# Other zero-products before the first product of h, and another order table, in a fused attention and MLP kernel

## The chip, the cores and the metric

The kernel runs on one core of one Trainium2 chip. The metric is the device time of one execution in microseconds. Before the change it is 183.79 us, the median of three runs (183.76 to 183.96). Less is better.

## The reference

The inputs are q, k and v of 8 batches, 8 heads, 576 positions and 64 columns, all in f32, and weights w_in (512 x 1024), w_out (1024 x 512), g_norm and g_ln. What is computed, cut to what matters:

```python
kv = np.einsum('bhsd,bhse->bhde', k, v)
out = np.einsum('bhsd,bhde->bhse', q, kv)
rms = np.sqrt(np.mean(out * out, axis=-1, keepdims=True) + 1e-06)
x = out / rms * g_norm                 # heads side by side: 4608 x 512
...
h = x @ w_in
e = np.exp(h - h_max)
solu = h * e / (np.sum(e) + 1e-09)
ln = (solu - mu) / np.sqrt(var + 1e-06) * g_ln
return ln @ w_out                      # 4608 x 512, f32
```

## The kernel before

The 4608 rows are worked in nine chunks c of 512 rows. Chunks 0 to 7 take eight of every nine positions of one batch each, chunk 8 the positions left over from all batches. A chunk goes through these pieces, by the names of the order table:

- `k`, `v`, `q`: loads from DRAM by GpSimd's DMA queue, with a cast to bf16 (line 281). For the first two batches they are split into parts: `k.0.1` is batch 0, part 1. `q_last` (line 296) loads the left-over positions. `w_in.0`, `w_in.1` (line 302) and `w_out` (line 307) load the weights. There are eight semaphores for these loads; the ninth load takes over the first one's and waits until that has landed, and so on.
- `kv_mm`: the products of k and v on TensorE (line 341); `kv`: their copies out of PSUM on VectorE or ScalarE (lines 191 and 193).
- `qT_mm` and `qT`: transposes of q on TensorE (line 366) and their copies. Later chunks are transposed by DMA instead (`q_turn`).
- `o_mm`: q times kv (line 394). `sq`: squares on ScalarE (line 402). `s_mm`: their means over a head on TensorE (line 408). `ex`, for other chunks `ln` and `ex`: one over the root on ScalarE (lines 422, 412, 416). `x`: the normed rows, on VectorE (line 434). In chunk 0 each of these four comes in four quarters, such as `sq.0.1.0`.
- `h_mm` (line 505, or `ht`, line 568, with rows and columns exchanged for chunks 5 to 8): x times w_in. `exp` or `et` on ScalarE, `u` or `ut` on VectorE, `usq` and `es` (squares of u, sums of e) mostly on GpSimd, `st` for the late chunks on VectorE or ScalarE.
- `sums`, `turn`, `stats`, `rstd`: the statistics of a row.
- `out` (line 696; the last tile in two halves of columns, `out.8.3.0` and `out.8.3.1`, line 705): u times the centred w_out. `ob`: scaled out of PSUM by VectorE or ScalarE (lines 711, 713). `store`: DMA of the result.

Two pieces prepare w_out: `w_mean`, eight products of 512 columns on TensorE that need all of w_out (line 681), and `w_center`, one per block of 128 rows on VectorE (line 684). `table` loads ScalarE's second function table.

`warm` (line 249) multiplies zeros by zeros into a PSUM bank that no one reads. `WARM` lists how many such products each `warm` piece has.

The order of all work is written out by hand in the string `ORDER`, read by `Plan.emit`: each word is a piece; `@dve`, `@act`, `@pool`, `@sp` choose an engine where there is a choice; behind `=` stand the buffers it takes (for a piece that writes PSUM the bank, 0 to 7). Pieces are issued in this order to the queue of their engine, and each engine works its queue in order. Within one engine the table alone decides; between engines, semaphores do.

Of the kernel before, what the change touches and what calls it, by code (L numbers as in the profile page):

```python
# [30 lines left out]
es.0.0=0 h_mm.0.7.0=5 u.0.4.0 exp.0.6.0=3 u.0.3.1 h_mm.0.4.1=2 exp.0.5.1 h_mm.0.5.0=7 usq.0.2@pool exp.0.4.1 u.0.5.1
h_mm.0.6.1=1 usq.0.1@act u.0.6.0 kv_mm.1.0=4 u.0.4.1 q.3.0=0 exp.0.6.1 w_center.1 qT_mm.1.0=0 exp.0.5.0 k.2.0=2
u.0.3.0 kv.1.0.1@act h_mm.0.7.1=2 kv.1.0.0@act qT.1.0@dve=1 exp.0.7.0 out.0.0.0=6 v.2.0=2 u.0.5.0 kv.1.0.2@act
exp.0.7.1 u.0.7.0 es.0.2 o_mm.1.0=04 w_center.6 out.0.2.0=7 sq.1.0.0=1 u.0.7.1 usq.0.5@act w_center.7 s_mm.1.0.0=5
usq.0.7@pool kv_mm.1.1=2 ln.1.0.0=0 u.0.6.1 qT_mm.1.1=3 sq.1.0.1=2 es.0.1 kv.1.1.1@dve kv.1.1.0@dve out.0.2.1
qT.1.1@dve kv.1.1.2@act ex.1.0.0=2 usq.0.4@pool s_mm.1.0.1=1 o_mm.1.1=52 ln.1.0.1=1 x.1.0.0=1 out.0.3.0=3 usq.0.3@pool
sq.1.1.1=0 out.0.0.1 sq.1.1.0=3 es.0.3 ex.1.0.1=0 s_mm.1.1.1=1 s_mm.1.1.0=0 ln.1.1.1=0 out.0.3.1 x.1.0.1 usq.0.6@pool
ln.1.1.0=1 qT_mm.2.0=1 ex.1.1.1=1 qT_mm.3.0=4 q.4.0=1 ex.1.1.0=2 sums.0=0 x.1.1.1 k.3.0=0 qT.3.0@act=2 x.1.1.0 v.3.0=0
qT_mm.2.1=2 turn.0 qT.2.0@act=3 h_mm.1.0=5 stats.0 q.5.0=2 rstd.0 qT.2.1@dve h_mm.1.2=4 q_last.5 exp.1.0=0
ob.0.0@dve=5 h_mm.1.1=0 exp.1.2=2 u.1.0=1 ob.0.3@act=0 qT_mm.3.1=1 ob.0.2@dve=3 kv_mm.2.0=26 exp.1.1 store.0.3 u.1.2  # L40
es.1.0=1 h_mm.1.6=5 kv.2.1.2@act kv.2.0.0@dve kv.2.1.1@act kv.2.0.2@dve kv.2.1.0@act kv.2.0.1@dve u.1.1 o_mm.2.0=37
exp.1.6=1 q_last.6 o_mm.2.1=46 qT.3.1@dve h_mm.1.3=2 sq.2.0.0=1 usq.1.0@pool=1 sq.2.1.1=2 u.1.6 s_mm.2.0.0=0
sq.2.0.1=0 qT_mm.4.0=1 usq.1.1@pool out.0.1.0=5 ln.2.0.0=0 qT.4.0@dve=0 v.4.0=1 exp.1.3 qT_mm.4.1=0 ex.2.0.0=0
s_mm.2.0.1=1 k.4.0=1 u.1.3 out.0.1.1 ln.2.0.1=1 x.2.0.0=2 usq.1.6@pool s_mm.2.1.1=2 sq.2.1.0=3 h_mm.1.4=1 ob.0.1@dve=2
ex.2.0.1=1 es.1.1 s_mm.2.1.0=3 ln.2.1.1=0 h_mm.1.5=5 x.2.0.1 ln.2.1.0=1 q_last.7 qT.4.1@dve h_mm.1.7=2 ex.2.1.1=2
ex.2.1.0=0 out.1.0.0=7 x.2.1.1 exp.1.4=3 x.2.1.0 kv_mm.3.0=30 exp.1.7 u.1.4 h_mm.2.0=6 usq.1.2@act es.1.3 kv.3.0.2@dve
kv.3.1.2@dve h_mm.2.2=4 u.1.7 exp.2.0=0 usq.1.3@pool kv.3.0.0@dve exp.1.5 h_mm.2.4=1 kv.3.1.1@dve kv.3.1.0@dve
exp.2.2=2 k.6.0=2 u.2.0=0 h_mm.2.1=2 exp.2.4=1 kv.3.0.1@dve es.1.2 u.1.5 o_mm.3.0=06 h_mm.2.3=3 u.2.2 sq.3.0.1=1
usq.2.0@pool=0 sq.3.0.0=0 u.2.4 h_mm.2.6=5 exp.2.3 usq.1.5@pool h_mm.2.7=4 exp.2.6=3 u.2.3 exp.2.1 usq.1.4@pool
s_mm.3.0.0=1 u.2.6 out.1.0.1 ln.3.0.0=0 u.2.1 v.6.0=2 exp.2.7 qT_mm.5.0=3 s_mm.3.0.1=5 ex.3.0.0=1 usq.1.7@pool  # L50
qT.5.0@dve=1 h_mm.2.5=1 ln.3.0.1=1 u.2.7 out.1.2.0=2 es.2.0=0 exp.2.5 x.3.0.0=0 ex.3.0.1=2 kv_mm.4.0=35 u.2.5
usq.2.2@pool usq.2.1@act x.3.0.1 o_mm.3.1=40 out.1.3.0=1 sq.3.1.1=2 kv.4.0.0@dve q.7.0=0 kv.4.0.2@dve sq.3.1.0=3
out.1.1.0=6 kv.4.1.1@dve k.5.0=0 kv.4.0.1@dve kv.4.1.0@act kv.4.1.2@act s_mm.3.1.1=3 usq.2.5@pool s_mm.3.1.0=5
out.1.2.1 ln.3.1.0=0 v.7.0=0 ln.3.1.1=1 out.1.3.1 ex.3.1.0=0 q_last.1 out.1.1.1 ex.3.1.1=1 x.3.1.0 v.5.0=1 usq.2.4@act
sums.1=5 x.3.1.1 es.2.2 h_mm.3.4=3 turn.1 usq.2.3@pool stats.1 h_mm.3.0=4 rstd.1 es.2.3 h_mm.3.6=0 ob.1.0@dve=4
exp.3.0=0 es.2.1 ob.1.1@dve=1 exp.3.4=1 store.1.0 h_mm.3.1=5 exp.3.6=3 u.3.0=1 qT_mm.5.1=7 store.1.1 usq.2.7@pool
ob.1.3@act=6 u.3.6 h_mm.3.7=6 qT.5.1@act ob.1.2@dve=7 q.6.0=1 h_mm.3.5=4 u.3.4 exp.3.1 store.1.2 usq.2.6@pool
out.2.3.0=1 exp.3.5 u.3.1 store.1.3 es.3.0=1 exp.3.7 o_mm.4.0=02 u.3.5 o_mm.4.1=73 sq.4.0.0=0 sums.2=5 u.3.7
sq.4.1.0=1 usq.3.0@pool=1 sq.4.0.1=2 s_mm.4.0.0=4 turn.2 out.2.3.1 es.3.3 ln.4.0.0=0 stats.2 s_mm.4.1.0=6 ex.4.0.0=2
out.2.2.0=5 rstd.2 x.4.0.0=1 out.2.1.0=4 ln.4.1.0=1 ob.2.3@dve=0 sq.4.1.1=3 out.2.2.1 ex.4.1.0=0 out.2.0.0=0  # L60
ob.2.2@dve=4 x.4.1.0 s_mm.4.1.1=6 s_mm.4.0.1=1 ln.4.1.1=0 out.2.0.1 ln.4.0.1=1 h_mm.3.3=5 ex.4.0.1=1 kv_mm.5.0=76
ex.4.1.1=2 x.4.0.1 h_mm.3.2=1 ob.2.0@act=1 kv.5.0.2@dve x.4.1.1 kv.5.0.0@act store.2.0 out.2.1.1 kv.5.1.2@dve
exp.3.2=2 qT.6=3 h_mm.4.0=2 u.3.2 exp.3.3 es.3.1 u.3.3 h_mm.4.1=0 exp.4.0=0 kv.5.1.0@act h_mm.4.2=3 u.4.0=0
usq.3.2@act qT.7=2 kv.5.1.1@dve usq.4.0@pool=0 ob.2.1@act=7 h_mm.4.4=1 kv.5.0.1@dve exp.4.2=3 h_mm.4.5=5 es.3.2
exp.4.1 exp.4.4=2 h_mm.4.3=2 store.2.3 u.4.1 usq.3.3@pool exp.4.5 u.4.4 o_mm.5.0=67 store.2.1 kv_mm.6.0=40 u.4.5
sq.5.0.0=0 usq.3.7@pool out.3.1.0=1 exp.4.3 kv.6.1.1@dve usq.4.1@pool sq.5.0.1=1 u.4.3 h_mm.4.6=5 u.4.2 usq.4.4@pool
h_mm.4.7=2 exp.4.6=1 kv.6.1.2@dve kv.6.0.2@dve es.4.0=0 usq.3.1@act kv.6.1.0@dve s_mm.5.0.0=3 out.3.1.1 u.4.6
usq.3.5@act kv.6.0.0@dve s_mm.5.0.1=0 usq.3.6@pool ln.5.0.0=1 kv.6.0.1@dve out.3.0.0=5 exp.4.7 usq.3.4@pool
out.3.2.0=4 ln.5.0.1=0 u.4.7 ex.5.0.0=0 out.3.0.1 usq.4.6@pool ex.5.0.1=1 x.5.0.0=2 o_mm.5.1=30 q_last.4 sums.3=2
x.5.0.1 sq.5.1.0=3 sq.5.1.1=2 k.7.0=1 s_mm.5.1.0=6 usq.4.7@act turn.3 es.4.1 out.3.3.0=7 stats.3 ln.5.1.0=1 out.3.2.1  # L70
ex.5.1.0=2 es.4.3 s_mm.5.1.1=2 rstd.3 x.5.1.0 out.3.3.1 ln.5.1.1=0 q_last.0 ob.3.1@dve=6 ht.5.0.0=6 ob.3.0@act=1
usq.4.2@pool ex.5.1.1=0 store.3.0 ht.5.1.0=3 et.5.0.0=00 q_last.3 x.5.1.1 ht.5.0.1=2 q_last.2 et.5.1.0=3 ut.5.0.0=1
ht.5.1.1=1 usq.4.3@pool et.5.0.1 ut.5.1.0 ht.5.3.0=5 et.5.1.1 ob.3.3@dve=0 es.4.2 ht.5.2.0=0 ut.5.0.1 et.5.3.0=1
usq.4.5@pool ht.5.3.1=6 ut.5.1.1 et.5.2.0=2 ut.5.3.0 uT.5.0=1 ht.5.2.1=3 et.5.3.1 ut.5.2.0 o_mm.6.1=72 et.5.2.1
o_mm.6.0=15 ut.5.3.1 sums.4=0 sq.6.1.0=0 ut.5.2.1 store.2.2 sq.6.0.0=1 ob.3.2@dve=7 out.4.1.0=6 sq.6.1.1=3 turn.4
s_mm.6.1.0=3 stats.4 out.4.2.0=4 uT.5.1 ln.6.1.0=1 st.5.2@dve=1 sq.6.0.1=2 s_mm.6.0.0=0 out.4.3.0=3 ln.6.0.0=0
st.5.0@dve=0 out.4.2.1 ex.6.0.0=1 ex.6.1.0=2 s_mm.6.0.1=0 x.6.0.0=0 out.4.3.1 rstd.4 x.6.1.0 out.4.1.1 ob.4.2@act=1
st.5.1@dve=1 ln.6.0.1=0 store.4.2 s_mm.6.1.1=1 ht.6.1.1=7 ln.6.1.1=1 st.5.3@dve=0 qT.8=0 ex.6.0.1=0 ht.6.0.0=4
ex.6.1.1=1 ht.6.0.1=0 x.6.0.1 et.6.0.0=01 x.6.1.1 ht.6.1.0=1 store.0.0 ob.4.3@dve=4 ht.6.2.0=5 et.6.1.0=3 ut.6.0.0=1
# [733 lines left out]
```

## Time and profile before

| | |
|---|---|
| median of three runs | 183.79 us |
| profiled execution, its own time | 184.49 us |
| its span, first to last instruction | 182.7 us |
| TensorE busy | 174.1 us, 95% |
| ScalarE busy | 146.1 us, 80% |
| VectorE busy | 127.1 us, 70% |
| GpSimd busy | 89.8 us, 49% |
| mean granted clock of TensorE | 0.98 |

The profile is of one execution. PE is TensorE's products, PEld its weight loads, DVE is VectorE, ACT ScalarE, POOL GpSimd, SP the engine that issues stores. L249 is line 249 of the kernel. In an answer by lines, "x48" is a count, and the mean of one follows in ns. A product's busy time includes its way through the array, so back-to-back products overlap; how often they start is read from groups that follow each other without a gap. The granted clock is TensorE's, 1.00 for full speed.

### The profile page before, as it was taken

How to read it: one execution, taken by the hardware profiler on the slowest of the kernel's cores; microseconds unless marked ns; L12 is line 12 of the kernel's file. 1: busy time of each engine (PE TensorE's matmuls, PEld its weight loads, DVE VectorE, ACT ScalarE, POOL GpSimd, SP SyncE). 2: the span in 40 equal slices, each digit the busy share in tenths (PEclk: the TensorE clock that was granted, in tenths of full speed). 3: DMA queues.
4: the chain of work that ended last, by engine and by line, in shares of the span. 5: the costliest groups of instructions: out<-in, count | busy, mean ns of one | idle time of the engine just before them, and what ended most of it. 6: DMA issues, size and time to landing. Idle time of an engine off the chain costs nothing.

```text
span 182.7 us, 4909 instructions
## 1 busy us (share of the span) xinstructions
PE 174.1 (95%) x1969; PEld 89.2 (49%) x1969; DVE 127.1 (70%) x298; ACT 146.1 (80%) x289; POOL 89.8 (49%) x104
## 2 busy tenths in 40 slices
...
GB/s 23 197 243 387 204 205 206 207 209 166 184 233 195 200 151 148 207 218 277 70 170 178 58 58 179 134 171 117 173 202 207 112 147 199 189 129 209 199 214 216
DMA packets 48551, 32.83 MB, mean 180 GB/s; under 512 B 28936, under 2 KB 43024, under 8 KB 48528
## 3 DMA queue, kind: packets, MB, share of 16 engines
...
q10 hardware_dynamic: 288, 0.39, 0.6%
...
## 4 chain that ended last, share of the span: by engine, by line
PE 89%; ACT 3%; DMA 3%; POOL 1%; issue 1%; DVE 1%; POOLq 0%
PE out_ps L696 32%; PE h_ps L505 19%; PE ht_ps L568 15%; PE kv_ps L341 4%; PE s_ps L408 4%; PE qT_ps L366 3%; PE sum_ps L652 3%; DMA q_sb<-in_q_dram 3%; PE warm_ps L249 3%; PE o_ps L394 3%; ACT osq_sb L402 2%; PE mean_ps L681 1%; PE acc_ps L705 1%; ACT lss_sb L412 1%; POOL v_sb L281 0%
## 5 line engine op out<-in xcount | busy, mean ns | idle before, releaser
L434 DVE SCALAR_TENSOR_TENSOR x_sb<-o_ps,g_rep,rst_sb 128x512 bf16<-128x512 f32 x36 | 26.0, 747 | 19.8 <-ACT rst_sb L416 15.1
L696 PE MATMUL out_ps<-w_out_sb,u_sb 128*128 128x512 bf16 x160 | 39.2, 379 | 0.0
L505 PE MATMUL h_ps<-x_sb,w_in_sb 128*128 128x512 bf16 (+1 forms) x192 | 37.4, 344 | 0.0
L531 POOL TENSOR_TENSOR usq_sb<-u_sb 128x512 bf16<-128x512 bf16 x31 | 31.9, 1042 | 4.9 <-DVE u_sb L520 4.8
L537 POOL TENSOR_TENSOR es_sb<-e_sb 128x512 bf16<-128x512 f32 x20 | 25.4, 1276 | 12.3 <-ACT e_sb L513 12.3
L513 ACT ACTIVATE e_sb<-h_ps,zero_t 128x512 f32<-128x512 f32 (+1 forms) x48 | 27.7, 621 | 4.0 <-PE h_ps L505 3.6
L520 DVE TENSOR_TENSOR u_sb<-h_ps,e_sb 128x512 bf16<-128x512 f32 (+1 forms) x48 | 27.2, 596 | 4.9 <-ACT e_sb L513 4.5
L568 PE MATMUL ht_ps<-w_in_sb,x_sb 128*128 128x512 bf16 x128 | 29.3, 379 | 0.2 <-ACT lss_sb L412 0.2
L696 PE MATMUL out_ps<-w_out_sb,usq_sb 128*128 128x512 bf16 x120 | 28.5, 379 | 0.0
L505 PEld LDWEIGHTS <-w_in_sb 128*128 128x128 bf16 x192 | 18.2, 98 | 15.0 <-issue 0.7
L578 ACT ACTIVATE e_sb<-ht_ps,zero_t 128x512 f32<-128x512 f32 x32 | 21.9, 692 | 3.6 <-PE ht_ps L568 2.8
L402 ACT ACTIVATE osq_sb<-o_ps,zero_t 128x512 bf16<-128x512 f32 x36 | 23.2, 689 | 1.6 <-PE o_ps L394 1.6
L696 PEld LDWEIGHTS <-u_sb 128*128 128x128 bf16 x160 | 15.2, 98 | 17.4 <-issue 0.6
L412 ACT ACTIVATE lss_sb<-s_ps,eps_t 128x512 f32<-128x512 f32 x32 | 21.6, 694 | 2.3 <-PE s_ps L408 2.2
L586 DVE SCALAR_TENSOR_TENSOR u_sb<-ht_ps,e_sb 128x512 bf16<-128x512 f32 x32 | 21.2, 686 | 2.1 <-ACT e_sb L578 1.8
L416 ACT ACTIVATE rst_sb<-lss_sb,zero_t 128x512 f32<-128x512 f32 x32 | 22.2, 733 | 0.2
L568 PEld LDWEIGHTS <-x_sb 128*128 128x128 bf16 x128 | 12.5, 98 | 15.6 <-issue 0.7
L696 PEld LDWEIGHTS <-usq_sb 128*128 128x128 bf16 x120 | 11.5, 98 | 13.5 <-issue 0.2
L193 DVE CAST kvd<-kv_ps 64x128 bf16<-64x128 f32 (+1 forms) x31 | 8.5, 287 | 13.2 <-PE kv_ps L341 12.8
L597 DVE SCALAR_TENSOR_TENSOR es_sb<-u_sb 128x1024 bf16<-128x1024 bf16 x13 | 15.5, 1218 | 0.0
L191 ACT CAST kvd<-kv_ps 64x128 bf16<-64x128 f32 (+1 forms) x17 | 4.5, 263 | 13.7 <-DVE kvd L193 11.6
L713 DVE TENSOR_SCALAR rooms<-out_ps,rstd 128x512 f32<-128x512 f32 x18 | 13.3, 745 | 1.8 <-PE out_ps L696 1.0
...
## 6 DMA issues: line engine op xcount, KB each, us to landing
...
w_out_f<-in_moe_w_out_dram POOLq DMA_DIRECT2D x1, 2048.0 KB, 12.2
...
```

The source lines that it names most:

```text
L402: nc.scalar.activation(out=t[:, :], in_=T[("o", *i)].rearrange("p a b c -> p (a b c)"), func=AF.Square, bias=zero_t[:, :])
L412: nc.scalar.activation(out=t[:, :], in_=T["s", i][:, :], func=AF.Ln, bias=eps_t[:, :])
L416: nc.scalar.activation(out=t.rearrange("p a b c -> p (a b c)"), in_=T["lss", i][:, :], func=AF.Exp, scale=-0.5, bias=zero_t[:, :])
L434: nc.vector.scalar_tensor_tensor(out=dst, in0=T["o", c, hf, z][:, :, :, :], scalar=g_rep[:, :], in1=T["rst", (c, hf, z)][:, :, :, :], op0= ...
L505: nc.tensor.matmul(t[:, :], w_in_sb[:, dt, f * 128:(f + 1) * 128], T["x", c][:, dt, cols_of(g)], start=(dt == 0), stop=(dt == NP - 1),)
L513: nc.scalar.activation(out=T["e", c, f // 2][:, f % 2, cols_of(g)], in_=T["h", c, f, g][:, :], func=AF.Exp, bias=zero_t[:, :])
L520: nc.vector.tensor_tensor(out=T["u", c][:, f, cols_of(g)], in0=T["h", c, f, g][:, :], in1=T["e", c, f // 2][:, f % 2, cols_of(g)], op=MUL)
L531: of(engine).tensor_tensor(out=dst, in0=src, in1=src, op=MUL)
L537: nc.gpsimd.tensor_tensor(out=T["es", c][:, n, :], in0=e[:, 0, :], in1=e[:, 1, :], op=ADD)
L568: nc.tensor.matmul(t[:, :], T["x", c][:, dt, 128 * m:128 * m + 128], w_in_sb[:, dt, 512 * w:512 * w + 512], start=(dt == 0), stop=(dt == N ...
L578: nc.scalar.activation(out=T["e", c, m][:, w, :], in_=T["ht", c, m, w][:, :], func=AF.Exp, bias=zero_t[:, :], accum_out=T["acc", c][:, 2 * ...
L696: nc.tensor.matmul(T["out", c, m][:, :], u_rows(c, f, m), w_out_sb[:, f, :], start=(f == 0), stop=(f == NF - 1),)
```

## The change

All 28 zero-products in 18 pieces become 44 in 9 pieces, and the whole order table is replaced. Nothing else is edited; the instructions that compute the result are the same in number.

```diff
-    WARM = (7, 2, 2, 2, 2, 1, 1, 1, 1, 1, 1, 1, 1, 1, 1, 1, 1, 1)
+    WARM = (14, 13, 2, 1, 1, 2, 5, 2, 4)
```

The table up to the first products of h:

```diff
-warm.0=7 v.0.0=0 k.0.0=0 q.0.0=0 ident k.0.1 q.0.2 v.0.1 q.0.1 q.0.3 w_out=01234567 warm.1=7 warm.2=7 qT_mm.0.0=0
-turn_g=1 w_in.0 w_in.1 k.1.0=1 warm.3=7 warm.4=7 qT_mm.0.2=2 kv_mm.0.0=3 v.1.0=1 kv.0.0.0@dve qT.0.0@dve=0
-kv.0.0.2@act warm.5=7 warm.6=7 kv_mm.0.1=4 q.1.0=1 qT.0.2@dve g_mean qT_mm.0.1=5 kv.0.1.2@act k.1.1 kv.0.1.0@act
-kv.0.0.1@dve qT.0.1@dve qT_mm.0.3=6 v.1.1 o_mm.0.0.0=70 qT.0.3@act kv.0.1.1@act warm.7=5 warm.8=5 o_mm.0.0.1
-o_mm.0.1.0=21 sq.0.0.1=0 o_mm.0.1.1 sq.0.0.0=1 sq.0.1.1=2 warm.9=4 warm.10=4 warm.11=4 s_mm.0.0.0=3 ex.0.0.0=0
-s_mm.0.1.1=5 s_mm.0.0.1=6 sq.0.1.0=3 x.0.0.0=0 ex.0.1.1=1 warm.12=4 warm.13=4 s_mm.0.1.0=4 ex.0.0.1=2 warm.14=7
-w_mean=3 q.1.1 ex.0.1.0=0 x.0.0.1 table x.0.1.0 x.0.1.1 w_center.5 warm.15=0 warm.16=2 warm.17=2 h_mm.0.0.0=7
...
+warm.0=7 v.0.0=0 ident v.0.1 q.0.0=0 k.0.0=0 k.0.1 q.0.2 q.0.3 q.0.1 w_out=01234567 w_in.0 w_in.1 warm.1=7 kv_mm.0.0=0
+v.1.0=1 qT_mm.0.0=1 kv.0.0.0@act qT.0.0@dve=0 kv.0.0.1@dve warm.2=7 kv_mm.0.1=2 k.1.0=1 qT_mm.0.2=3 q.1.0=1
+kv.0.1.1@act kv.0.0.2@act qT.0.2@dve kv.0.1.0@act warm.3=1 o_mm.0.0.0=45 v.1.1 turn_g=6 kv.0.1.2@act qT_mm.0.3=7
+qT_mm.0.1=1 k.1.1 qT.0.3@dve o_mm.0.1.0=03 qT.0.1@dve g_mean warm.4=2 o_mm.0.0.1 o_mm.0.1.1 sq.0.0.0=0 sq.0.1.1=1
+warm.5=1 s_mm.0.0.0=2 ex.0.0.0=0 sq.0.1.0=2 x.0.0.0=0 sq.0.0.1=3 warm.6=6 s_mm.0.1.0=7 ex.0.1.0=1 s_mm.0.0.1=1
+s_mm.0.1.1=6 x.0.1.0 ex.0.1.1=2 warm.7=4 w_mean=2 q.1.1 x.0.1.1 table x.0.0.1 w_center.7 w_center.2
+warm.8=5 h_mm.0.0.0=4 q.3.0=2 w_center.5 h_mm.0.2.0=7 exp.0.0.0=0 h_mm.0.2.1=6 w_center.4 exp.0.2.0=1 h_mm.0.0.1=0
...
```

On TensorE, 11 zero-products stood ahead of the first real product before (the transposes `qT_mm.0.0`); now 27 stand ahead of it (`kv_mm.0.0`). The other 17 are spread between there and the first `h_mm` in both tables. On GpSimd the eight loads of batch 0 that come ahead of w_out are in another order, with `ident` second instead of fourth. Behind `w_in.1` the loads of batch 1 begin with v instead of k, then `q.3.0` comes ahead of `q.2.0`, and `v.2.0` now stands ahead of the first `usq`.

From there on the same pieces follow in another order, with other banks and here and there another engine. The end of the table:

```diff
-store.7.3 rstd.8 out.8.0.1 ob.8.1@act=4 store.7.2 out.8.2.0=4 ob.8.0@act=3 out.8.3.0=5 store.8.0@sp out.8.2.1
-ob.8.3.0@dve=5 store.8.3.0@sp out.8.3.1=0 ob.8.2@act=2 store.8.1@sp store.8.2@act ob.8.3.1@dve store.8.3.1@act
+store.7.2 out.8.2.0=3 ob.7.3@dve=1 ob.8.1@dve=5 out.8.3.0=4 store.7.3 store.8.1@act out.8.2.1 ob.8.3.0@dve=4
+store.8.3.0@act out.8.3.1=2 ob.8.2@dve=0 store.8.2@act ob.8.3.1@dve store.8.3.1@sp
```

More of the change, by code (lines that the diff above doesn't have):

```diff
@@ L31 @@
[L31 to L79, printed above, removed]
-store.3.3 ht.6.3.0=2 stats.5 et.6.1.1 ut.6.1.0 out.5.2.0=3 et.6.0.1 ut.6.1.1 out.5.3.0=4 et.6.2.0=1 ut.6.0.1 rstd.5
@@ new lines @@
+usq.0.4@pool ln.1.1.1=1 qT_mm.3.1=7 ex.1.1.0=0 qT_mm.3.0=0 q.4.0=1 ex.1.1.1=1 sums.0=5 x.1.1.0 v.3.0=0 qT.3.0@act=2
+x.1.1.1 k.3.0=0 qT_mm.2.0=2 turn.0 h_mm.1.6=1 stats.0 v.4.0=1 qT.3.1@dve rstd.0 q_last.5 h_mm.1.0=0 qT.2.0@dve=3
+ob.0.0@act=7 h_mm.1.2=5 ob.0.3@dve=2 exp.1.0=0 ob.0.2@act=5 qT_mm.2.1=7 u.1.0=1 h_mm.1.1=2 exp.1.2=1 qT.2.1@dve
+exp.1.6=2 u.1.2 kv_mm.2.0=43 exp.1.1 h_mm.1.3=6 kv.2.1.1@dve kv.2.0.1@act es.1.0=1 kv.2.0.0@dve kv.2.1.0@act
+kv.2.0.2@dve kv.2.1.2@act u.1.6 o_mm.2.1=07 exp.1.3 o_mm.2.0=53 q.5.0=2 u.1.1 out.0.1.0=4 sq.2.1.1=0 k.4.0=1
@@ new lines @@
+sq.3.1.0=3 usq.2.4@pool s_mm.3.1.1=0 s_mm.3.1.0=7 ln.3.1.1=0 out.1.2.1 k.6.0=0 ln.3.1.0=1 es.2.3 out.1.1.0=0
+ex.3.1.0=2 sums.1=7 ex.3.1.1=0 usq.2.7@pool x.3.1.0 x.3.1.1 out.1.1.1 v.6.0=1 turn.1 usq.2.1@pool stats.1 h_mm.3.4=1
+rstd.1 es.2.1 h_mm.3.0=4 usq.2.3@act ob.1.3@dve=0 kv.4.1.1@act h_mm.3.6=7 ob.1.1@dve=1 store.1.3 exp.3.0=0
+usq.2.5@pool h_mm.3.7=3 u.3.0=1 exp.3.6=1 usq.2.2@pool ob.1.0@dve=3 usq.2.6@act h_mm.3.5=0 u.3.6 exp.3.4=3 q_last.7
+store.1.0 qT_mm.5.1=4 exp.3.7 u.3.4 h_mm.3.1=6 q.6.0=1 kv.4.1.2@act store.0.0 exp.3.5 kv.4.1.0@dve sums.2=7 u.3.7
```

82 lines of the change are left out of this document (61 added, 21 removed).

## The prediction

> **What bounds the kernel now.** I read the page first, then the chain of waits from its end backwards, then the body as one stretch, then the landings of the loads and the clock by stretches.
>
> ```profile
> PE 174.1 (95%) x1969; PEld 89.2 (49%) x1969; DVE 127.1 (70%) x298; ACT 146.1 (80%) x289; POOL 89.8 (49%) x104
> ```
>
> TensorE is busy for 95% of the span, far more than any other engine, so the question is where its other 5% lie and whether its busy time is work at its best rate. The chain of waits (start, length, what) answers both:
>
> ```profile
> 15.22 0.34 PE qT_ps L366 x4
> 15.56 0.02 issue
> 15.59 0.44 DVE qT_sb L193
> ...
> 17.16 1.85 ACT osq_sb L402 x3
> ...
> 20.36 0.39 PE s_ps L408
> 20.75 0.22 PE warm_ps L249
> 20.96 1.84 PE mean_ps L681 x8
> 22.80 0.46 PE warm_ps L249 x2
> 23.27 0.04 issue
> 23.31 0.38 PE warm_ps L249
> 23.69 6.64 PE h_ps L505 x60
> ...
> 166.05 10.36 PE out_ps L696 x48
> ...
> 178.15 0.89 PE acc_ps L705 x8
> ```
>
> Up to the first product of h the chain goes back and forth between ACT, TensorE and loads; from there on it stays on TensorE nearly throughout. 48 products of 512 columns take 10.36 us there, 216 ns each, with no gap between them. The stretch from the first h (its instruction starts at 23.52 in the timeline quoted below) to the end of the last product (178.15 + 0.89, about 179.03):
>
> ```profile
> 23.52:179.03 155.51, 155.30 (x1809) 80.46 (x1807) 120.49 (x274) 137.21 (x274) 75.22 (x78) 1.00 0.97 175
> ```
>
> In 155.51 us TensorE is busy 155.30 (the columns are length, then PE, PEld, DVE, ACT, POOL, the clock, DMA). So the body is its products back to back, at full clock (1.00). The time of the kernel is then (start of the first h) + 155.5 + the tail, 182.7 - 179.03 = 3.7 us. Another order of the same products cannot shorten the body by more than that 0.2 us and the small cost of changing shapes; what it can do is start the body sooner, or put waits into it.
>
> **The change part by part.** *The head.* The first h needs three things: w_in's first half, x's first two quarters, and, by its place behind w_mean on TensorE, w_out. When do they land?
>
> ```profile
> L307 POOL DMA_DIRECT2D w_out_f<-in_moe_w_out_dram x1: 944/944/944, 7.9 to 7.9; - x1
> ...
> DMA to landing us min/median/max: 12.2/12.2/12.2
> ```
>
> ```profile
> L302 POOL DMA_DIRECT2D w_in_sb<-in_moe_w_in_dram x1: 804/804/804, 8.8 to 8.8; - x1
> ...
> DMA to landing us min/median/max: 13.3/13.3/13.3
> ```
>
> w_out is here at 7.9 + 12.2 = 20.1, w_in.0 at 8.8 + 13.3 = 22.1. In both tables the same eight loads with the same bytes, and ident, stand ahead of w_out on POOL's queue, only permuted. So these two landings stay, give or take 0.2 us. Before, w_mean did not start at 20.1: TensorE came to it only behind the last s_mm, which waited for a square on ACT until 20.36, and a zero-product. From there, 8 products of w_mean took 1.84 us and three zero-products with their waits 0.88 (22.80 to 23.69).
>
> Is TensorE ready for w_mean by 20.1 in the changed table? Its first product is kv_mm.0.0, which needs the first and the fourth load; the last of the eight is q.0.1. The fourth and the eighth load of before had the same bytes ahead of them:
>
> ```profile
> L281 POOL DMA_DIRECT2D k_sb<-in_k_dram x1: 713/713/713, 4.4 to 4.4; - x1
> ...
> DMA to landing us min/median/max: 5.5/5.5/5.5
> ```
>
> ```profile
> L281 POOL DMA_DIRECT2D q_sb<-in_q_dram x1: 748/748/748, 7.2 to 7.2; - x1
> ...
> DMA to landing us min/median/max: 6.2/6.2/6.2
> ```
>
> So kv_mm.0.0 can start at 9.9 and the last transposes of q at 13.4. The 27 zero-products now ahead of kv_mm.0.0 fit in front of it:
>
> ```profile
> 1.20 4.65 PE L249 MATMUL warm_ps<-zeros 128*128 128x512 bf16 x11 [1.20 <-DVE zeros L212]
> 8.60 0.61 PE L366 MATMUL qT_ps<-ident,q_sb 128*128 128x128 bf16 x4 [2.75 <-DMA q_sb<-in_q_dram]
> ...
> 23.52 0.71 PE L505 MATMUL h_ps<-x_sb,w_in_sb 128*128 128x256 bf16 x5
> ```
>
> Eleven of them took 4.65 us, 423 ns each, twice the 216 of the body. If the clock comes after about 3.6 us, 8 slow and 19 fast ones end at 1.2 + 3.4 + 4.1 = 8.7; if all 27 stayed slow, at 12.6. I take 8.7 to 10.5, so between no delay and 0.6 us.
>
> From 13.4 on: four transposes and the copy on DVE took 0.34 and 0.44 us in the chain; with some 0.6 for waits and the sixteen small products of o_mm (an estimate; they are shorter than the 216 ns products) ACT's first square starts near 14.8 to 14.9. ACT then has eight operations in a row, four squares and four rsqrts. Three squares took 1.85 us in the chain, with 0.69 for the last to finish, so 0.58 apart. The fifth of the eight is the last square and ends near 14.9 + 4 x 0.58 + 0.69 = 17.9; its s_mm and two zero-products bring TensorE to w_mean at 18.7. The eighth ends near 19.7 and the x that waits for it (0.75 on DVE, by the 745 ns of the last row quoted in this part) at 20.5, ahead of h. So TensorE now waits 1.4 us for w_out, and all delays in the head up to 1.4 us are covered by that wait. That the first 27 zero-products, the earlier ident on POOL and the later k.0.0 cost nothing rests on this cover; without it each would count in full.
>
> Then: w_mean starts at 20.15, 1.84 us, four zero-products of warm.8 at 216 ns, 0.86 us: 22.85 to 22.9. w_in.0 has been there since 22.1. The first h starts at 22.9 instead of 23.52: **0.6 us gained**. Bounds: 0 (TensorE at w_mean only at 20.75 again) and 0.85 (w_out 0.2 earlier).
>
> *The body.* The same products, so 155.5 us. POOL now issues v.2.0 ahead of its first usq, and that load waits until an earlier one has landed, since it takes over its semaphore; es and the other usq queue behind it. POOL is busy 75 of 155 us in the body, and what it makes is first needed by sums of batch 0, so this is hidden; uncovered it is one issue, 0.71 us. Which places of the new order leave ACT (137 of 155 us busy) or DVE (120) late I bound from the rows: at best the idle 0.2 us of the stretch vanishes, at worst two operations of ACT (0.69 each) come late in full, 1.4 us. I take 0, since nearest to the row of before.
>
> *The tail.* ob.8.2 moves from ACT to DVE, between the two halves of ob.8.3.
>
> ```profile
> 179.06 0.48 DVE L713 TENSOR_SCALAR rooms<-acc_ps,rstd 128x256 f32<-128x256 f32 x1 [1.20 <-PE acc_ps L705]
> ```
>
> ```profile
> L713 DVE TENSOR_SCALAR rooms<-out_ps,rstd 128x512 f32<-128x512 f32 x18 | 13.3, 745 | 1.8 <-PE out_ps L696 1.0
> ```
>
> Its product ends at 178.15, where acc_ps begins in the chain, and DVE stood idle for 1.20 us before 179.06; 0.745 fits in with 0.1 to spare. Cost 0; if not covered, up to 0.5 us. The last store leaves from SP instead of ACT, taken as equal.
>
> *Sum.* 182.7 - 0.6 + 0 + 0 = 182.1 us of span. The profiled execution took 184.49 us by its own time, 1.8 around its span, and the median of the runs is 183.79, 0.7 below it. The difference carries over: **183.79 - 0.6 = 183.2 us**.
>
> **The rivals.** *A, the body starts no sooner (about 183.8).* For it: k.0.0 is now the fourth load instead of the second, and the chain behind it (kv, copies, o_mm, squares) has to make up 2 us. Against it: before, nothing used that early landing; kv_mm.0.0 stood behind two transposes and ran at half clock, and ACT's squares began only at 17.16. It takes a slip of 1.4 us before the gain begins to shrink and 2.0 before it is gone.
>
> *B, slower: the clock falls while TensorE waits for w_out.* By stretches of before (length, PE busy and count, and so on; the clock is the number behind POOL):
>
> ```profile
> 4.82:8.24 3.42, 0.97 (x4) 0.20 (x2) 0.00 (x0) 0.00 (x0) 3.42 (x6) 1.00 1.24 193
> 8.24:11.65 3.41, 3.00 (x13) 1.42 (x13) 0.00 (x0) 0.00 (x0) 3.41 (x5) 0.50 1.27 202
> 11.65:15.07 3.42, 3.36 (x77) 2.16 (x74) 2.00 (x6) 0.26 (x1) 2.64 (x4) 0.50 1.32 346
> ```
>
> A stretch with 0.97 us of work in 3.42 was followed by half clock; the next, with 3.00, did not end it, and the one with 3.36 did (the stretch of the body above stands at 1.00). The changed kernel's 3.4 us up to 20.2 hold perhaps 1.9 us by the same records (four s_mm and some five zero-products, each with its row longer than its 216 ns), between the first of these and the last. If the clock falls there, 3.4 us of w_mean, warm.8 and the first h run at half speed and lose 1.7 us: 183.2 + 1.7 = 184.9. It decides from 0.6 us lost, that is, from 1.2 us at half clock. The Trainium skill, "TensorE: Matmul & The Clock Gate" (Why this matters for your kernels), asks for no idle gap over about 3 us; by it the gap of 1.4 us is harmless, B would have no chance, and the time would stay at 183.2. The trace does not quite agree: the gap in which the clock fell here was 2.75 us long (the bracket of the row at 8.60), below that figure. So I leave B one chance in ten.
>
> *C, slower: the new order makes ACT or DVE late in the body.* ACT's 137 of 155 us leave little room and where one operation is late TensorE's queue stands behind it. Against it: the old order, as dense, leaves TensorE idle for 0.2 us only. At 1.4 us: 183.2 + 1.4 = 184.6; it decides from 0.6 us of waits.
>
> **How the numbers follow.** Forecast 0.58, A 0.20, B 0.10, C 0.12. The forecast's own range is 182.6 to 183.5 (0.85 to 0.3 gained in head and body). About 0.2%, 0.37 us, is what can be told from no change here. The forecast is nearly all below that line; A is no change; B and C are slower: faster 0.58, same 0.21, slower 0.21. To leave out no more than two in ten the range goes from 182.5 to 184.5, which takes in A and the lighter half of C.
>
> **What would show it right or wrong.** Right: TensorE idle for about 1.4 us ahead of mean_ps, released by the DMA of w_out_f near 20.1; the first h at 22.9; full clock from the first stretch on; some 155.5 us from the first h to the last product; 3.7 us behind it. Wrong: squares on ACT starting after 16.5; a clock of 0.50 anywhere between 16 and 25; h not before 23.4; named waits of TensorE in the body adding up to over 0.6 us.

## The result and the profile after

| | before | after |
|---|---|---|
| median of the runs, us | 183.77 | 186.49 |
| profiled execution, its own time, us | 184.49 | 185.57 |
| its span, us | 182.7 | 183.8 |
| first h, us | 23.52 | 22.98 |
| end of the last product, us | 179.03 | 178.44 |
| tail behind it, us | 3.67 | 5.36 |
| mean granted clock | 0.98 | 1.00 |

The changed kernel is slower by 1.4%: ratio 1.0141, 95% interval 1.0103 to 1.0179. Its profiled execution is the fastest of its runs, 0.9 us below their median, so part of the loss does not stand in this trace at all. The ratios of all kernels leave out three executions that were over 1.5% above the fastest of the same kernel: 187.24 and 187.33 us with the gap filled, 186.53 us with ident back (both kernels are described below).

First the head, from the timeline of TensorE in the changed kernel (start, length, what; in brackets the idle time ahead of it and what ended it):

```profile
7.66 1.89 PE L248 MATMUL warm_ps<-zeros 128*128 128x512 bf16 x8
11.28 0.75 PE L340 MATMUL kv_ps<-v_sb,k_sb 64*64 64x64 bf16 x36 [1.73 <-DMA k_sb<-in_k_dram]
...
16.84 0.38 PE L407 MATMUL s_ps<-osq_sb,head_mean 128*128 128x512 bf16 x1
...
20.15 2.11 PE L680 MATMUL mean_ps<-w_out_f,g_mean 128*128 128x512 f32 x8
22.11 1.04 PE L248 MATMUL warm_ps<-zeros 128*128 128x512 bf16 x4
22.98 1.25 PE L504 MATMUL h_ps<-x_sb,w_in_sb 128*128 128x256 bf16 x10
```

The first h is where it was forecast (22.98 against 22.9), and behind w_out's landing, as forecast. But the gap is in another place: TensorE stands for 1.73 us ahead of kv_mm.0.0, because k.0.0 landed at 11.2 and not at 9.9, and not for 1.4 us ahead of w_mean. The chain of waits in the changed kernel has both ends of this:

```profile
4.39 6.84 DMA k_sb<-in_k_dram
...
20.18 2.09 PE mean_ps L680 x8
```

TensorE comes to w_mean at 20.18 instead of the forecast 18.7, just behind w_out's landing at 20.1. The late k.0.0 has used up the whole cover of 1.4 us, and the first h is on time with nothing to spare.

The body and the tail, as stretches (length, then PE, PEld, DVE, ACT, POOL busy, clock, DMA share, GB/s), in the changed kernel:

```profile
22.98:178.44 155.46, 155.35 (x1809) 80.21 (x1807) 121.53 (x271) 137.12 (x276) 76.86 (x80) 1.00 0.96 174
```

```profile
178.44:183.80 5.36, 0.00 (x0) 0.00 (x0) 0.48 (x1) 0.00 (x0) 0.00 (x0) 0.93 0.55 185
```

and the tail of the kernel before:

```profile
179.03:182.70 3.67, 0.00 (x0) 0.00 (x0) 0.48 (x1) 0.00 (x0) 0.00 (x0) 0.95 0.52 193
```

The body is 155.46 us, the forecast's 155.5. Behind it the changed kernel still has 5.36 us x 185 GB/s = 0.99 MB to move, the kernel before 3.67 x 193 = 0.71. The 0.28 MB between them are about two DMAs of 128 KB. The queue of SP in the changed kernel shows where they come from:

```profile
164.23 4.14 SPq L743 DMA_DIRECT2D out_dram<-rooms  x6
168.47 2.12 SPq L601 DMA_TRANSPOSE usq_sb<-u_sb  x1
170.69 4.15 SPq L743 DMA_DIRECT2D out_dram<-rooms  x6
174.93 0.54 SPq L738 DMA_DIRECT2D out_dram<-rooms  x1
175.58 2.66 SPq L743 DMA_DIRECT2D out_dram<-rooms  x4
178.99 0.34 SPq L725 DMA_DIRECT2D out_dram<-rooms  x1
```

and in the kernel before:

```profile
165.22 3.67 SPq L744 DMA_DIRECT2D out_dram<-rooms  x6
168.99 2.08 SPq L602 DMA_TRANSPOSE usq_sb<-u_sb  x1
171.57 5.04 SPq L744 DMA_DIRECT2D out_dram<-rooms  x8
176.70 0.54 SPq L739 DMA_DIRECT2D out_dram<-rooms  x1
```

L743 (L744 before) is a store of chunks 0 to 7, two DMAs of 128 KB each. By the two tables, the eight DMAs that SP issues in the kernel before from 171.57 on are the four stores of chunk 7. In the changed kernel ten are issued from 170.69 on, and two more just ahead of the transpose: among them are store.5.3 at 173.6, whose rows were ready since 135.9, and store.5.1 at 167.1 (ready since 137.5). SP issues one in some 0.6 us, so the four cost it 2.4 us, and the last DMA of chunk 7 leaves at 177.4 instead of 176.0. ACT issues its own stores at 176.4, 177.3 and 178.4 into the same stretch. What this makes of the transfers, by the rows of the last stores in the changed kernel:

```profile
L743 SPq DMA_DIRECT2D out_dram<-rooms x4: 486/567/847, 175.6 to 177.4; - x4
...
DMA to landing us min/median/max: 2.8/3.0/4.5
```

and in the kernel before:

```profile
L744 SPq DMA_DIRECT2D out_dram<-rooms x5: 548/587/592, 173.4 to 176.0; - x5
...
DMA to landing us min/median/max: 2.3/2.4/2.4
```

From issue to landing the slowest takes 4.5 us instead of 2.4.

### The profile page after: what moved, and what is told of

Same layout as the page of the kernel before. It is cut to its first block, busy times and chain, and to the rows that moved or that the text cites. A ratio compares the mean times of both kernels' runs of the same rounds, so it can differ in the third digit from the quotient of the medians.

```text
span 183.8 us, 4936 instructions
## 1 busy us (share of the span) xinstructions
PE 174.7 (95%) x1985; PEld 89.7 (49%) x1985; DVE 129.0 (70%) x295; ACT 145.8 (79%) x291; POOL 90.6 (49%) x105
## 4 chain that ended last, share of the span: by engine, by line
PE 86%; ACT 4%; DMA 4%; POOL 2%; issue 1%; DVE 0%; POOLq 0%
PE out_ps L695 32%; PE h_ps L504 19%; PE ht_ps L567 15%; PE s_ps L407 4%; PE kv_ps L340 4%; DMA k_sb<-in_k_dram 4%; PE sum_ps L651 3%; PE qT_ps L365 3%; PE o_ps L393 3%; ACT osq_sb L401 3%; PE warm_ps L248 1%; PE mean_ps L680 1%; PE acc_ps L704 1%; POOL v_sb L280 1%; ACT lss_sb L411 1%
## 5 line engine op out<-in xcount | busy, mean ns | idle before, releaser
L504 PE MATMUL h_ps<-x_sb,w_in_sb 128*128 128x512 bf16 (+1 forms) x192 | 36.6, 344 | 0.0
L530 POOL TENSOR_TENSOR usq_sb<-u_sb 128x512 bf16<-128x512 bf16 x32 | 32.8, 1042 | 0.8 <-PE h_ps L504 0.7
L401 ACT ACTIVATE osq_sb<-o_ps,zero_t 128x512 bf16<-128x512 f32 x36 | 22.8, 688 | 1.6 <-PE o_ps L393 1.5
L712 DVE TENSOR_SCALAR rooms<-out_ps,rstd 128x512 f32<-128x512 f32 x24 | 17.5, 747 | 7.9 <-PE out_ps L695 6.4
L415 ACT ACTIVATE rst_sb<-lss_sb,zero_t 128x512 f32<-128x512 f32 x32 | 22.5, 728 | 0.5
L411 ACT ACTIVATE lss_sb<-s_ps,eps_t 128x512 f32<-128x512 f32 x32 | 21.4, 691 | 1.8 <-PE s_ps L407 1.3
L695 PEld LDWEIGHTS <-usq_sb 128*128 128x128 bf16 x120 | 11.6, 98 | 14.2 <-DVE x_sb L433 0.6
L192 DVE COPY qT_sb<-qT_ps 128x1024 bf16<-128x1024 bf16 (+1 forms) x13 | 7.7, 604 | 12.3 <-PE qT_ps L365 12.3
L190 ACT CAST kvd<-kv_ps 64x128 bf16<-64x128 f32 (+1 forms) x25 | 6.5, 260 | 12.0 <-PE kv_ps L340 11.7
L248 PE MATMUL warm_ps<-zeros 128*128 128x512 bf16 x44 | 13.1, 438 | 1.3 <-DVE zeros L211 1.2
## 6 DMA issues: line engine op xcount, KB each, us to landing
q_sb<-in_q_dram POOLq DMA_DIRECT2D x6, 512.0 KB, 11.6
```

The source lines that it names most:

```text
L401: nc.scalar.activation(out=t[:, :], in_=T[("o", *i)].rearrange("p a b c -> p (a b c)"), func=AF.Square, bias=zero_t[:, :])
L411: nc.scalar.activation(out=t[:, :], in_=T["s", i][:, :], func=AF.Ln, bias=eps_t[:, :])
L415: nc.scalar.activation(out=t.rearrange("p a b c -> p (a b c)"), in_=T["lss", i][:, :], func=AF.Exp, scale=-0.5, bias=zero_t[:, :])
L504: nc.tensor.matmul(t[:, :], w_in_sb[:, dt, f * 128:(f + 1) * 128], T["x", c][:, dt, cols_of(g)], start=(dt == 0), stop=(dt == NP - 1),)
L530: of(engine).tensor_tensor(out=dst, in0=src, in1=src, op=MUL)
L695: nc.tensor.matmul(T["out", c, m][:, :], u_rows(c, f, m), w_out_sb[:, f, :], start=(f == 0), stop=(f == NF - 1),)
```

## The experiments

The twelve kernels ran in three groups of four, each with its own runs of the kernel before on the same chip: medians 184.03, 184.21 and 183.98 us. Ratios are to those.

### The same kernel again, and the two stores early

The first kernel is the changed one, not edited. In the second two words are moved:

```diff
-... out.7.3.0=1 store.5.1 st.8.0@act=0 ...
-... rstd.8 store.5.3 out.8.1.1 ...
+... store.4.0 store.5.1 store.5.3 x.7.1.0 ...
```

> The changed kernel once more, unedited, for a second trace and the scatter of its runs: its profiled span was 183.8 us, but the other runs had 184.6 to 184.9. Theory (the tail): the last product of TensorE again ends near 178.4, the first h again starts near 23.0, and the span differs from run to run by what lies behind the last product (5.3 us in the trace at hand, 3.7 before). Rival (the clock or the head): in a slower run the first h starts later than 23.0, by the half-speed time, and the tail stays at 5.3 us or below.

> The changed kernel with the stores of batch 5 that its table puts among the last ones (store.5.1 and store.5.3, four DMAs of 128 KB) moved up behind store.4.0, where the issuing engine stands idle from 142 to 148 us. Theory (stores pile up in the tail): with 256 KB and 1.2 us of issues less behind 173.6 us, the tail falls from 5.3 to about 3.7 us, the profiled span to about 182.1 us, and the time by at least 1.1 us, to 185.4 or below; to 183.2 if the slower runs too come from there. Rival (the head or the body costs the time): the tail may shrink, but the time stays within 0.4 us of 186.5.

Measured: the same kernel 186.64 us, ratio 1.0130 (1.0106 to 1.0153). Its profiled execution is again the fastest of its runs, 185.51 us. In it the first h starts at 23.38, 0.4 us later than in the first trace, at full clock and behind w_out's landing at 20.5; the last product ends at 178.83, and the tail is 4.90 us. The slower executions left no trace, so theory and rival are not decided by this kernel.

With the two stores early the time is 185.31 us, 1.0073 (1.0053 to 1.0092). The stretch behind the last product there:

```profile
179.75:183.49 3.74, 0.00 (x0) 0.00 (x0) 0.48 (x1) 0.00 (x0) 0.00 (x0) 0.94 0.50 168
```

The tail is back at 3.74 us and 3.74 x 168 = 0.63 MB, and the time falls by 186.64 - 185.31 = 1.3 us. So the two stores cost that. But the kernel is still slower than before by 0.7%, and its first h comes only at 24.29: there is a second loss, in the head.

### Heads exchanged

The pieces and zero-products up to the first h are taken from the one kernel and all behind them from the other, with some PSUM banks renamed: the kernel before with the changed head, and the changed kernel with the head of before.

```diff
-warm.0=7 v.0.0=0 k.0.0=0 q.0.0=0 ident k.0.1 q.0.2 ... w_mean=3 ... warm.17=2 h_mm.0.0.0=7
+warm.0=7 v.0.0=0 ident v.0.1 q.0.0=0 k.0.0=0 k.0.1 ... w_mean=3 ... warm.8=2 ... h_mm.0.0.0=7
```

> The kernel before with the changed kernel's order up to the first product of h (44 zero-products, the loads in the new order; bank numbers exchanged where the two tables collide) and its own order from there on. Theory: the head gains and the rest of the table loses, so the first h starts at 23.0 instead of 23.5 and the time falls by about 0.5 us, to 183.2 to 183.4. Rival (the zero-products cost the time): 184.5 or more.

> The changed kernel with the order of before up to the first product of h (28 zero-products, the loads in the old order) and the new order from there on. Theory: the body and the tail are those of the changed kernel, and they start 0.5 us later: 187.0 us, tail still over 5 us. Rival (the new head costs the time): near 183.8 us.

Measured: the kernel before with the changed head 184.85 us, 1.0040 (1.0021 to 1.0060): the head that was to gain 0.6 us loses 0.8. That is the rival's number, but not its cause: the kernel with the loads back, below, has the same 44 zero-products and is no slower than the kernel before. The changed kernel with the old head 186.08 us, 1.0098 (1.0072 to 1.0123), tail 5.97 us. That is 0.6 us less than with its own head, where 0.5 us more was expected. What happens in the changed head is seen by its stretches. The clock changes only at steps of 3.41 us. Here are stretches cut at those steps: first the kernel before with the changed head, the stretch with the gap ahead of kv_mm.0.0 and the next,

```profile
7.73:11.14 3.41, 1.21 (x6) 0.36 (x4) 0.00 (x0) 0.00 (x0) 2.65 (x4) 1.00 1.14 177
11.14:14.56 3.42, 3.04 (x75) 2.50 (x78) 0.72 (x2) 0.27 (x1) 2.39 (x4) 0.50 1.36 272
```

then the same two in the kernel with the stores early,

```profile
8.96:12.38 3.42, 1.53 (x44) 1.00 (x43) 0.00 (x0) 0.15 (x1) 2.20 (x3) 1.00 1.18 170
12.38:15.79 3.41, 3.05 (x54) 1.82 (x52) 1.14 (x3) 1.16 (x5) 2.65 (x4) 0.50 1.33 319
```

and in the profiled execution of the changed kernel:

```profile
8.97:12.38 3.41, 1.68 (x44) 1.07 (x43) 0.00 (x0) 0.27 (x1) 2.20 (x3) 1.00 1.28 191
12.38:15.79 3.41, 3.38 (x73) 2.12 (x72) 1.97 (x6) 1.04 (x4) 2.81 (x4) 1.00 1.31 364
```

With 1.68 us of products in the stretch the clock stays, with 1.53 it is halved for the whole next one. The gap ahead of kv_mm.0.0 is 2.23, 1.89 and 1.73 us long in these three, and the last two lie on either side of the edge, so the head is not the same from one execution to the next. The Trainium skill, "TensorE: Matmul & The Clock Gate" (Part 1: The HAM clock gate), describes such a free-running window of 3413 ns, and the stretches agree with it. The advice of the Trainium skill, "TensorE: Matmul & The Clock Gate" (Why this matters for your kernels), to leave no idle gap over about 3 us, is not strict enough here: a gap of 1.89 us cost the clock.

What the fall costs can be read from the mean granted clock that every execution has on record. In the traces it is 0.995 or more where the clock did not fall in the head, and 0.991 or less where it did. Of the twelve executions of the kernel before with the changed head, six have 0.995 or more and took 184.2 to 184.8 us; six have 0.990 or less and took 184.9 to 186.1, by the medians 0.8 us more. So in that kernel a fallen clock goes with some 0.8 us more.

The clock is not the whole loss of the head, though. The changed kernel has eight executions without a trace in its two sets of runs. Four of them have 0.997 or more and took 186.4 to 187.0 us, four have 0.982 to 0.985 and took 186.4 to 186.7; the two with a trace, both at full clock, took 185.6 and 185.5. What makes those eight some 1 us slower is not shown. One candidate stands in the trace with the stores early, in the weight load of w_mean (PEld):

```profile
21.44 1.70 PEld L678 LDWEIGHTS mean_ps<-w_out_f,g_mean 128*128 128x128 f32 x8 [0.38 <-DMA w_out_f<-in_moe_w_out_dram]
```

There w_out itself landed only at 21.4, so that first h at 24.29 would have come hardly earlier at full clock. In the kernel before with the changed head w_out was there at 20.6 and nothing waited for it; its first h at 24.10 is late by the clock.

### The loads, ident and the gap

Three kernels on top of the one with the two stores early. In the first the loads of batch 0 go back to about the order of before, in the second ident alone does, in the third the gap is filled by more zero-products:

```diff
-warm.0=7 v.0.0=0 ident v.0.1 q.0.0=0 k.0.0=0 k.0.1 q.0.2 q.0.3 q.0.1 w_out=01234567
+warm.0=7 v.0.0=0 k.0.0=0 q.0.0=0 ident v.0.1 k.0.1 q.0.2 q.0.3 q.0.1 w_out=01234567
```

```diff
-warm.0=7 v.0.0=0 ident v.0.1 q.0.0=0 k.0.0=0 k.0.1
+warm.0=7 v.0.0=0 v.0.1 q.0.0=0 ident k.0.0=0 k.0.1
```

```diff
-    WARM = (14, 13, 2, 1, 1, 2, 5, 2, 4)
+    WARM = (14, 22, 2, 1, 1, 2, 5, 2, 4)
```

> The changed kernel with store.5.1 and store.5.3 behind store.4.0 again, and with the loads of batch 0 as v.0.0 k.0.0 q.0.0 ident v.0.1 k.0.1 q.0.2 q.0.3 q.0.1. Theory (the head is lost where k.0.0 lands behind the fill, because ident stands second): k.0.0 lands at about 7.9 as in the kernel before, kv_mm.0.0 starts where the fill ends, 9.5 to 9.8, with no wait of over 0.5 us ahead of it and no fall of the clock; w_out lands at about 20.1, the first h starts at 22.9, the last product ends at 178.4, the tail is 3.7: span 182.1, and the time 0.4 to 0.7 us below the kernel before. Rival (the landing of w_out sets the head, and it comes late whatever the order of the small loads is when the batch-0 loads are crowded by other work): w_out lands at 20.5 to 21.4, h at 23.3 to 24.3, time 0 to 1.3 us above the kernel before.

> The changed kernel with the two stores early, and ident moved from second to fourth place, the loads else in the changed order. Theory (ident alone delays every small load behind it by 1.2 us): the second load lands at 7.9 instead of 9.1, k.0.0 at 9.95 instead of 11.2, kv_mm.0.0 starts at 10.0 after a wait of about 0.4 us, no fall of the clock; w_out at 20.1, h at 22.9, time 0.4 to 0.7 us below the kernel before. Rival (the landings are set by the bytes and by the queue, not by ident): k.0.0 still lands after 10.8, the wait stays at 1.2 us or more, and the time is that of the kernel with the two stores early alone, 1.3 us above the kernel before.

> The changed kernel with the two stores early, and warm.1 of 22 zero-products instead of 13, so that the 1.7 to 1.9 us gap ahead of kv_mm.0.0 is filled. Theory (the gap lets the clock fall in some executions, and that is what makes the head unsteady): no record below 1.00 between 6 and 180, kv_mm.0.0 starts at 11.3 to 11.6, the first s product at 16.8, the spread of the runs is under 0.4 us, and the time is 0.5 to 1.0 us below that of the kernel with the two stores early alone. Rival (the landing of w_out sets the first h, the clock does not): w_mean waits for w_out_f at 20.4 to 21.4 also at full clock, and the time stays within 0.3 us of the kernel with the two stores early alone.

Measured: loads back 183.72 us, 0.9977 (0.9960 to 0.9994). Ident back 183.82 us, 0.9976 (0.9956 to 0.9996). Gap filled 184.75 us, 1.0031 (1.0011 to 1.0051). TensorE with the loads back:

```profile
17.89 0.59 PE L246 MATMUL warm_ps<-zeros 128*128 128x512 bf16 x2
19.94 2.14 PE L678 MATMUL mean_ps<-w_out_f,g_mean 128*128 128x512 f32 x8 [1.45 <-DMA w_out_f<-in_moe_w_out_dram]
21.91 1.04 PE L246 MATMUL warm_ps<-zeros 128*128 128x512 bf16 x4
22.79 6.71 PE L502 MATMUL h_ps<-x_sb,w_in_sb 128*128 128x256 bf16 x60
```

This is the head that the prediction described: a wait of 1.45 us for w_out ahead of w_mean (forecast 1.4), w_mean at 19.94, h at 22.79, full clock throughout. It is faster than the kernel before by 0.2%, on the edge of what can be told. Moving ident alone does as much as moving all the loads. Filling the gap keeps the clock, and gains 1.0073 - 1.0031 = 0.4% on the kernel with the two stores early alone, some 0.8 us, as its theory said. That the kept clock is what gains it is likely but not shown: the one execution with the stores early that kept the clock (1.000) took 185.45 us, no less than the others. The other 0.5% up to the kernel with the loads back is not taken apart. In the trace with the gap filled k.0.0 lands at 10.05, but the fill holds TensorE until 11.6, and the first h starts at 23.15 instead of 22.79. That its runs would lie within 0.4 us of each other was wrong: those compared go from 184.1 to 185.4.

### The other way round: late stores and ident second in the kernel before

```diff
-... store.6.0 ... store.6.1 ... store.6.2 ... store.7.1 ... store.7.0 ...
+... store.6.0 ... store.7.1 store.6.1 ... store.7.0 store.6.2 ...
```

```diff
-warm.0=7 v.0.0=0 k.0.0=0 q.0.0=0 ident k.0.1
+warm.0=7 v.0.0=0 ident k.0.0=0 q.0.0=0 k.0.1
```

> The kernel before with two stores of chunk 6 moved into the tail: store.6.1 behind store.7.1, store.6.2 behind store.7.0. Nothing else is edited. Theory (four late issues of 0.6 us on SP push the last stores together, and these then land later): the last product still ends at 179.0, store.8.1 leaves SP 1 to 1.5 us later than 178.7, the last transfers take 3.5 us or more from issue to landing, the tail grows from 3.7 to between 4.8 and 6.2 us, time 1.1 to 2.5 us above the kernel before. Rival (late stores are absorbed by the free time on SP, and the long tail of the changed kernel is of another cause): tail within 0.4 us of 3.7, time within 0.4 us of the kernel before.

> The kernel before with ident moved from fourth to second place among POOL's first pieces. Nothing else is edited. Theory (in most executions the load behind ident lands about 1.4 us later, and those behind it with it): k.0.0 lands at about 9.1 instead of 7.9, the first transposes of q start at 9.8 instead of 8.6, the first s product about 1 us later than 18.5, first h 23.8 to 24.6, time 0.3 to 1.1 us above the kernel before. Rival (ident's place does not matter; the new order of k and v behind it did): k.0.0 at 7.5 to 8.0, time within 0.3 us of the kernel before.

Measured: stores late 186.37 us, 1.0121 (1.0096 to 1.0147). SP and the tail in it:

```profile
167.63 1.94 SPq L601 DMA_TRANSPOSE usq_sb<-u_sb  x1
170.83 7.52 SPq L743 DMA_DIRECT2D out_dram<-rooms  x12
178.45 0.54 SPq L738 DMA_DIRECT2D out_dram<-rooms  x1
```

```profile
178.28:184.21 5.93, 0.00 (x1) 0.00 (x0) 0.48 (x1) 0.10 (x1) 0.00 (x0) 0.95 0.69 223
```

Twelve DMAs in a row, 5.93 x 223 = 1.32 MB left behind the last product, a tail of 5.93 us, and 2.2 us more time than the kernel before: the tail and the time that the theory gave, in a kernel in which nothing else was touched.

Ident second alone: 184.90 us, 1.0044 (1.0025 to 1.0062), 0.9 us slower. That is the theory's time, but the profiled execution (184.21, among the fastest of its runs) does not show the theory's landing: from issue to landing the second load took 4.8 us there, and landed at 7.8. Over all profiled executions, as issue plus time to landing, with the places of ident:

| | ident second | ident fourth |
|---|---|---|
| second load lands at, us | 9.1, 9.3, 9.1, 9.0, 7.5, 7.8 | 7.9, 7.7, 7.6, 7.5, 7.5, 7.5, 8.1, 7.8 |
| w_out lands at, us | 20.1, 20.5, 21.4, 20.6, 20.1, 20.4 | 20.1, 20.0, 20.0, 19.9, 19.8, 19.7, 19.9, 19.8 |

With ident second the second load lands at 9.0 to 9.3 in four of six, instead of 7.5 to 8.1, though it is issued only 0.8 us later, and w_out lands on average at 20.5 instead of 19.9, though it is issued at the same 7.9. The row of the second load in the changed kernel,

```profile
L280 POOL DMA_DIRECT2D v_sb<-in_v_dram x1: 719/719/719, 3.0 to 3.0; - x1
...
DMA to landing us min/median/max: 6.2/6.2/6.2
```

beside the one in the kernel with the filled gap, with the same order of loads:

```profile
L278 POOL DMA_DIRECT2D v_sb<-in_v_dram x1: 722/722/722, 3.0 to 3.0; - x1
...
DMA to landing us min/median/max: 4.6/4.6/4.6
```

The fourth load, issued at 4.4 in every kernel, shows it too: it lands at 9.5 to 10.2 with ident fourth, and with ident second at 11.1 to 11.4 in four traces and at 10.05 and 10.35 in the other two. The late second load reaches further: w_in.0 takes over its semaphore, so in those four it is issued at 9.3 to 9.6 instead of 8.8, and lands at 22.5 to 23.8; with ident fourth it lands at 22.1 to 22.4. Why a load issued at 2.96 takes 6.1 to 6.3 us in four traces and 4.6 and 4.8 in two is not settled.

### One loss or two, the rest of the body, and a shorter fill

Only the loads mended, with the stores late as the change has them (the first diff of the loads above, alone). Then the changed kernel with the head of before and the two stores early. Last, the kernel with loads and stores mended and a shorter fill ahead of the first h:

```diff
-    WARM = (14, 13, 2, 1, 1, 2, 5, 2, 4)
+    WARM = (14, 13, 2, 1, 1, 2, 5, 2, 1)
```

> The changed kernel with only the loads of batch 0 put as v.0.0 k.0.0 q.0.0 ident v.0.1 k.0.1 q.0.2 q.0.3 q.0.1; the late stores stay as the change has them. Theory (two separate losses that add up: the load order costs 1.5 us in the head, the two late stores 1.2 to 2 us in the tail): kv_mm.0.0 at about 9, first h at 22.8, last product at 178.3, tail 5 to 5.6 us, time 1.2 to 2 us above the kernel with both parts mended, that is 0.8 to 1.6 us above the kernel before and 0.8 to 1.6 below the changed one. Rival (they are one loss: the long tail only follows from an unsteady head): tail under 4.2 us and the time within 0.5 us of the kernel with both mended.

> The changed kernel with the head of the kernel before (its pieces, order and zero-products up to the first h) and store.5.1 and store.5.3 early. Theory (the body costs the same in both tables, and all of the loss is the head and the two stores): first h at 23.1 to 23.5, last product 178.7 to 179.1, tail 3.7, time within 0.4 us of the kernel before. Rival (something in the new body still costs): last product later than 179.5 or the time more than 0.6 us above the kernel before.

> The changed kernel with both parts mended (loads of batch 0 in the new order, store.5.1 and store.5.3 early) and the last fill ahead of the first h cut from 4 zero-products to 1. Theory (ahead of the first h TensorE works off 4 zero-products after w_in's first half has landed at 22.2 to 22.3): the first h starts when w_in.0 lands, 22.2 to 22.4 instead of 22.7 to 22.8, no fall of the clock, time 0.3 to 0.5 us below the kernel with both mended. Rival (w_in.0 lands later than the zero-products end, or x is late): first h within 0.1 us of 22.75, time within 0.15 us.

Measured: loads only 185.23 us, 1.0070 (1.0052 to 1.0088); its first h is at 22.55, its tail 4.97 us. Old head and early stores 184.02 us, 1.0017 (0.9997 to 1.0038), with this body:

```profile
22.70:178.17 155.47, 154.10 (x1789) 80.13 (x1807) 121.67 (x271) 137.24 (x276) 76.91 (x80) 1.00 0.97 176
```

Shorter fill 183.26 us, 0.9962 (0.9948 to 0.9976):

```profile
19.93 2.11 PE L678 MATMUL mean_ps<-w_out_f,g_mean 128*128 128x512 f32 x8 [0.81 <-DMA w_out_f<-in_moe_w_out_dram]
21.88 0.39 PE L246 MATMUL warm_ps<-zeros 128*128 128x512 bf16 x1
22.30 2.36 PE L502 MATMUL h_ps<-x_sb,w_in_sb 128*128 128x256 bf16 x20
```

Four kernels now stand as a square, by their ratios:

| | two stores late | two stores early |
|---|---|---|
| loads as changed | 1.0141 | 1.0073 |
| loads mended | 1.0070 | 0.9977 |

The stores cost 0.7 to 0.9% (1.3 to 1.7 us), the head 0.7 to 1.0% (1.3 to 1.8 us), and each costs that with and without the other: two losses that add up, as far as the intervals tell. The body costs the same 155.5 us in both tables (155.4 to 155.6 in all fourteen traces), and with the old head and early stores the changed body is no different from the kernel before. The kernel with both mended and the shorter fill is faster than the kernel before by 0.4% (0.7 us) and beats both. Against the one with four zero-products its interval overlaps; the trace shows the gain where it was expected, the first h at 22.30 instead of 22.79, just behind w_in's first half:

```profile
L299 POOL DMA_DIRECT2D w_in_sb<-in_moe_w_in_dram x1: 804/804/804, 8.8 to 8.8; - x1
...
DMA to landing us min/median/max: 13.4/13.4/13.4
```

8.8 + 13.4 = 22.2.

## Why the prediction was wrong

Forecast 183.2 us, measured 186.49, 3.3 us more, outside the range. By its steps:

- *The body, 155.5 us:* right, 155.45 to 155.63 in the changed table whatever stood ahead of it. C did not happen. That POOL's v.2.0, the banks and the changed engines cost nothing there was right too, to within some 0.1 us.
- *The tail, 3.7 us unchanged:* this is the first step that failed. The prediction looked at the last stores only ("the last store leaves from SP instead of ACT, taken as equal") and at ob.8.2. It did not count what else the new table had put on SP's queue ahead of them: store.5.1 and store.5.3, four issues of 0.6 us. Their rows had been ready for some 30 us and more, so no wait pointed at them. Measured 5.36 us, +1.7 in the profile (4.9 to 6.0 us in the other traces with late stores), 1.3 to 1.7 us by the experiments, and +2.2 us when the same is done to the kernel before.
- *"The fourth and the eighth load of before had the same bytes ahead of them":* this is the second. The bytes are the same, and so is the time of issue, 4.4, but ident stands ahead of seven of the loads instead of five. In four of the five traces with the changed order of loads k.0.0 lands at 11.1 to 11.4, not 9.9. The earlier ident was counted as covered by the wait for w_out. The cover held in the profile, to its last 0.1 us, but the delay opened a gap ahead of kv_mm.0.0 on the edge at which the clock falls. Where it falls, TensorE comes to w_mean at 21.45 instead of 20.18 and to the first h at 24.10 (the kernel before with the changed head). The loss in the head is 1.3 to 1.8 us by the experiments, and ident alone, put back, ends it; how much of it goes by the clock and how much by late landings of w_out and w_in.0 stays open.
- *w_out at 20.1 and w_in.0 at 22.1, "give or take 0.2 us":* 20.1 to 21.4 and 22.5 to 23.8 with ident second.
- *B:* the mechanism happens, a clock that falls after a stretch with too little work, but ahead of kv_mm.0.0, where the prediction put its 27 zero-products "between no delay and 0.6 us". They ended in time; the load was late.
- *A and the reference, "the difference carries over":* also wrong. The first h at 23.52 belongs to an execution 0.7 us above the median. With the old head other executions have it at 23.14, 22.87 and 22.70. The one at 22.87, in the kernel with the stores late, already waits for w_out:

```profile
20.03 2.12 PE L680 MATMUL mean_ps<-w_out_f,g_mean 128*128 128x512 f32 x8 [0.41 <-DMA w_out_f<-in_moe_w_out_dram]
```

So most of the 0.6 us to be gained was not there in the median execution: 183.77 - 1.8 - 155.5 - 3.7 = 22.8 for its first h, by the prediction's own terms. What the mended head gains is 0.2%, 0.4 us.

The sum of the misses: 0.7 (the profiled execution before above its median, which did not carry over) + 1.7 (tail) + 0.9 (the median execution of the changed kernel above the profiled one) = 3.3 us. No trace shows the last term; a first h near 23.9 instead of 22.98 would account for it, and the traces of the changed head with a fallen clock or a late w_out have 24.1 and 24.3. The changed table as printed ahead of the prediction lacks a word of the kernel, `ex.0.0.1=0` behind `w_mean=2`; with it there are the four rsqrts that the prediction counts.
